# One PSUM pool, tile 0's output projection ahead of tile 1's value sums, one load for the shift and scale weights, and a longer per-tile tail in the last group

## The chip, the cores and the metric

The kernel runs on one core of one Trainium2 chip. The metric is device time in microseconds: the median of three runs of the kernel before is 567.99 us (566.24 to 569.38). Engines are named as in the profile: PE is TensorE (PEld its weight loads), DVE is VectorE, ACT is ScalarE, POOL is GpSimd, SP is SyncE, which here only issues DMAs.

## What is computed

A transformer block with adaptive layernorm on 2048 tokens of width 576, in bf16. From the reference, shortened:

```
mod = silu(c) @ w_mod                      # six rows of 576: sa, ca, ga, sb, cb, gb
h = layernorm(x) * (1 + ca) + sa
x = x + ga * A(h)                          # sliding attention: 32 heads of 18, 8 keys two apart
h = layernorm(x) * (1 + cb) + sb
x = x + gb * ((h @ w_gate) * (h @ w_up)) @ w_down       # 4608 inner columns
```

## The kernel before

Tokens are worked in 16 tiles of 128, two of which make a chunk of 256 for the attention. The feed-forward part runs over five groups of tiles, `GROUPS = [(0, 2), (2, 6), (6, 10), (10, 13), (13, 16)]`; in each, `gate_up` makes the product `hh` of 36 row tiles of the inner width (line L630 for its matmuls), and `down` sums it against `w_down`. The attention of later chunks is cut into pieces and placed between the matmuls of earlier groups. Every engine's order is the order in which the program is written (`manual_schedule`); no planner moves anything. Waits come from the data and from buffers that must be free again.

Three places matter here.

**The start.** `load_wm` loads the weights of one row of `mod` as columns: a 128-partition DMA for four chunks of the width and a 64-partition DMA for the last (L167, L168). It is called twice for `wmA`, for the shift and for the scale of the first layernorm. `mod_columns(wmA, 0)` multiplies them with silu(c) on PE (`pm`, L292: 25 matmuls for the shift, 25 for the scale); between the two stand 16 matmuls on zeros (`run_idle`, L183), whose result nobody reads. The evictions of the first transposes into `hT` need the result (`modc`); the first projections `pq` (L347) read `hT` and the weights `wqk`.

**The hand-over to the first group.** For chunk 0 the weighted values are summed on PE: `av_sum(j, hf)` (L516) sums half of the keys for tile j into three PSUM tiles `po`, and after the second half ACT copies that tile's columns to `oT` (L519 to L521). `b_wj(j)` multiplies them with Wo (`pwj`, L530); its result, called later, lets DVE add the residual and take the statistics of the second layernorm (L536, L537, L240). `rsq2` is that layernorm's Ln and Exp on ACT, `norm2` its normalization on DVE (L250), `transposed(xn2, ...)` its transposes on PE (L277) and their evictions, which split over DVE and ACT and end in `h2T`. Between these stand the projections of chunk 2: `a_q(2, g)` (L347) and `a_v(2, j)` (L373, L375; evicted to `v_sb` by ACT, L377, L378, and stored by POOL). In the kernel before, both tiles' sums stand ahead of Wo of tile 0. The PSUM tiles come from two pools: `pop` with three banks for `po` and the idle matmuls, and a pool of five for all others. Ahead of the first group both are closed and one of eight banks is opened, so that the first `pg` waits until all old banks are released.

**The end.** `down` of the last group has three tiles. For each row tile f of the inner width it runs, for each tile, one matmul of 512 columns into `acc` (two of 256 for the last tile; L697) and one of 64 columns into `accr` (L701). The loop stops at `last`:

```
        last = FT - FB                       # 36 - 4
        for f in range(last):
            for j in range(nj):
                mm_a(f, j)
                mm_r(f, j)
            if f % FB == FB - 1:
                load_wd(gi * NBLK + f // FB + 3)
```

The down weights come in nine blocks of four row tiles (`load_wd`, L164, issued by POOL), through three buffers. Block 8 goes into the buffer of block 5 and is issued after row tile 23. After the loop the remaining row tiles are run by kind: first all `accr` of all tiles, then tile by tile the `acc` (L728), each followed by its multiplication with `gb_bc` on DVE (L729), its addition to the residual (L731; on POOL for the first two tiles, on DVE for the last) and its store (L733).

Of the kernel before, what the change touches and what calls it, by code (L numbers as in the profile page):

```python
# [8 lines left out]
F32 = mybir.dt.float32  # L9
ALU = mybir.AluOpType  # L10
ACTF = mybir.ActivationFunctionType
AX = mybir.AxisListType
PSUM = bass.MemoryType.PSUM
# [5 lines left out]
P = 128  # L19
D = 576  # L20
DP = 640
KT = 5
KF = 4
# [5 lines left out]
FT = FF // P  # L29
# [3 lines left out]
CH = 256  # L33
ST = CH // P
NB = 512
FB = 4
# [7 lines left out]
def kernel(  # L44
# [13 lines left out]
    nc = tc.nc  # L58
# [6 lines left out]
    def pool(name, bufs, **kw):  # L65
        return ctx.enter_context(tc.tile_pool(name=name, bufs=bufs, **kw))
# [18 lines left out]
    wdp = pool("wdp", 3)  # L85
    gup = pool("gup", 3)
    outr = pool("outr", 1)
    guards = [tc.tile_pool(name="pop", bufs=3, space=PSUM), tc.tile_pool(name="psp0", bufs=5, space=PSUM)]
    pop, psp = [g.__enter__() for g in guards]

    def ps(shape, dt, name):
        return psp.tile(shape, dt, name=name, tag="bank")

    def js(j):
        return slice(j * P, (j + 1) * P)
# [70 lines left out]
    def load_k(dst, wsrc, c0, n):  # L166
        r = nc.sync.dma_start(dst(slice(0, P), slice(0, KF)), wsrc[0:KF * P, c0:c0 + n].rearrange("(k p) n -> p k n", p=P))  # L167
        nc.sync.dma_start(dst(slice(0, 64), KF), wsrc[KF * P:D, c0:c0 + n])  # L168
        return r

    def load_wm(wm, bi, blk):
        return load_k(lambda p, k: wm[p, k, bi, :], w_mod, blk * D, D)

    x_in[0] = sp.tile([P, ST, D], BF, name="x_t0")
    for j in range(ST):
        nc.sync.dma_start(x_in[0][:, j, :], x_flat[js(j), :])
    zero = sp.tile([P, P], BF, name="zero")
    nc.vector.memset(zero[:], 0.0)
    idle = pop.tile([P, 2, CH], F32, name="po")

    def run_idle(n):
        for _ in range(n):
            nc.tensor.matmul(idle[:, 0, 0:P], lhsT=zero[:], rhs=zero[:], start=True, stop=True, skip_group_check=True)  # L183

    c_row = sp.tile([KT, P], BF, name="c_row")
    nc.vector.memset(c_row[:], 0.0)
# [11 lines left out]
    wmCr = x1p.tile([P, D], BF, name="x1")  # L198
    nc.gpsimd.memset(wmA[64:, KF, :, :], 0.0)
    nc.gpsimd.memset(wmCr[64:, :], 0.0)  # L200
    load_wm(wmA, 0, 0)
    load_wm(wmA, 1, 1)
    load_k(lambda p, k: wqk[p, k, 0:D], A_wqkv, 0, D)
    load_k(lambda p, k: wqk[p, k, D:DP], A_wqkv, 2 * D - 64, 64)
    load_k(lambda p, k: wqk[p, k, DP:2 * D], A_wqkv, D, D - 64)
# [79 lines left out]
    def mod_columns(wm, pi):  # L285
        pm = ps([P, 2, KT], F32, "pm")
        for bi in range(2):
            if pi == 0 and bi == 1:
                run_idle(16)
            for kt in range(KT):  # L290
                for m in range(KT):
                    nc.tensor.matmul(pm[:, bi, m:m + 1], lhsT=wm[:, kt, bi, col(m)], rhs=sc[:, kt:kt + 1],  # L292
                                     start=(bi == 0 and kt == 0 and m == 0), stop=(kt == KT - 1), skip_group_check=True)
        c01 = slice(2 * pi, 2 * pi + 2)
        nc.vector.tensor_tensor(modc[:, c01, 0:KF], pm[:, :, 0:KF], addc[:, :, 0:KF], ALU.add)
        for r in (slice(0, 64), slice(64, P)):
            nc.vector.tensor_tensor(modc[r, c01, KF:KT], pm[64:P, :, KF:KT], addc[64:P, :, KF:KT], ALU.add)
# [59 lines left out]
    def a_q(i, g):  # L357
        qk_tiles(i, QGRP[g], slice(0, CH), nc.scalar.copy)
        if g == 2:
            a_halo(i)  # L360
# [146 lines left out]

    def av_sum(j, hf):
        if j == 0 and hf == 0:
            pos.extend(pop.tile([P, 2, CH], F32, name="po") for _ in range(3))  # L510
        v = weighted[j][:].rearrange("p w d h -> p w (d h)")
        r = DIL * (W - 1) if j == 0 else 0
        for w in range(4 * hf, 4 * hf + 4):
            sh = DIL * (W - 1 - w)
            for m in range(KT):
                nc.tensor.matmul(pos[m // 2][:, m % 2, j * P:(j + 1) * P + r], lhsT=v[:, w, col(m)], rhs=slide[:, P - sh:2 * P - sh + r],  # L516
                                 start=(j == 0 and w == 0 and m % 2 == 0), stop=(w == W - 1), skip_group_check=True)
        if hf == 1:
            nc.scalar.copy(oT[:, 0:2, js(j)], pos[0][:, :, js(j)])  # L519
            nc.scalar.copy(oT[:, 2:4, js(j)], pos[1][:, :, js(j)])  # L520
            nc.scalar.copy(oT[0:64, KF, js(j)], pos[2][64:P, 0, js(j)])  # L521
# [162 lines left out]
    def down(gi, hh, bg):  # L684
        t0, t1 = GROUPS[gi]
        nj = t1 - t0
        last = FT - FB
        at = spread([(1.0, p) for p in bg], last)
        final = gi == NG - 1
        acc = [ps([P, 512], F32, "acc") for _ in range(nj - final)]  # L690
        halves = [(ps([P, CH], F32, "acc"), slice(CH * h, CH * (h + 1))) for h in range(2)] if final else []
        accr = ps([P, 2 * ST, 64], F32, "accr")

        def mm_a(f, j):
            wb = wd_blk[gi * NBLK + f // FB]
            for a, cs in [(acc[j], slice(0, 512))] if j < len(acc) else halves:
                nc.tensor.matmul(a[:], lhsT=hh[:, f, js(j)], rhs=wb[:, f % FB, cs], start=(f == 0), stop=(f == FT - 1))  # L697

        def mm_r(f, j):
            wb = wd_blk[gi * NBLK + f // FB]  # L700
            nc.tensor.matmul(accr[:, j, :], lhsT=hh[:, f, js(j)], rhs=wb[:, f % FB, 512:D],  # L701
                             start=(f == 0 and j == 0), stop=(f == FT - 1), skip_group_check=True)
# [7 lines that stand above are left out]
            for piece in at[f]:  # L710
                piece()
        xs = [x1[t // ST][t % ST] for t in range(t0, t1)]
        for j in range(nj):
            for f in range(last, FT):
                mm_r(f, j)
        o_ts = [gup.tile([P, 512], BF, name="o_t", tag="g_sb" if j % 2 else "u_sb") for j in range(nj)]
        t_r = outr.tile([P, 2 * ST, 64], BF, name="t_r")
        nc.vector.tensor_tensor(t_r[:, 0:nj, :], accr[:, 0:nj, :],
                                gb_bc[:, None, 512:D].to_broadcast([P, nj, 64]), ALU.mult)
        if final:  # L720
            for j in range(nj):
                nc.vector.tensor_tensor(xs[j][:, 512:D], t_r[:, j, :], xs[j][:, 512:D], ALU.add)
            for j in range(nj):
                r0 = (t0 + j) * P
                for a, cs in [(acc[j], slice(0, 512))] if j < nj - 1 else halves:
                    for f in range(last, FT):
                        wb = wd_blk[gi * NBLK + f // FB]
                        nc.tensor.matmul(a[:], lhsT=hh[:, f, js(j)], rhs=wb[:, f % FB, cs], start=False, stop=(f == FT - 1))  # L728
                    nc.vector.tensor_tensor(o_ts[j][:, cs], a[:], gb_bc[:, cs], ALU.mult)  # L729
                    adder = nc.gpsimd if j < nj - 1 else nc.vector  # L730
                    adder.tensor_tensor(xs[j][:, cs], o_ts[j][:, cs], xs[j][:, cs], ALU.add)  # L731
                    stored = slice(0, CH) if cs.stop == CH else slice(cs.start, D)
                    nc.sync.dma_start(out_flat[r0:r0 + P, stored], xs[j][:, stored])  # L733
            return
        for j in range(nj):
            for f in range(last, FT):
                mm_a(f, j)
            nc.vector.tensor_tensor(o_ts[j][:], acc[j][:], gb_bc[:, 0:512], ALU.mult)
        for j in range(nj):
            r0 = (t0 + j) * P  # L740
            nc.vector.tensor_tensor(xs[j][:, 0:512], o_ts[j][:], xs[j][:, 0:512], ALU.add)
            nc.vector.tensor_tensor(xs[j][:, 512:D], t_r[:, j, :], xs[j][:, 512:D], ALU.add)
            nc.sync.dma_start(out_flat[r0:r0 + P, :], xs[j][:])
        load_wd(gi * NBLK + NBLK + 2)
# [30 lines left out]
    nc.gpsimd.tensor_copy(sc_bc[:], sc[:, :, None].to_broadcast([P, KT, P]))  # L775
    run_idle(24)
    ev = [transposed(xn0, lambda m, j=j: hT0[:, m, js(j)], (j,), 0) for j in range(ST)]
    mod_columns(wmA, 0)
    for e in ev:
        e()  # L780
# [42 lines left out]
    load_x(2)  # L823
    wmB = sp.tile([P, KT, 2, D], BF, name="wmB", tag="wm")
    nc.gpsimd.memset(wmB[64:, KF, :, :], 0.0)
    load_k(lambda p, k: wmB[p, k, :, :].rearrange("p k b n -> p k (b n)") if k != KF else wmB[p, k, :, :].rearrange("p b n -> p (b n)"), w_mod, 3 * D, 2 * D)
    for dd4 in range(4):
        nk = (DH - dd4 + 3) // 4
        wsrc = bass.AP(A_wo.tensor, A_wo.offset + dd4 * D, [[DH * D, H], [4 * D, nk], [1, D]])
# [59 lines left out]
    xn2, stat2, rsq2, norm2 = ln_parts(lambda j: x1[0][j], "b")  # L889
    ht, _ = h2_of(0)  # L890
    a_q(2, 1)
    av_sum(1, 0)
    a_q(2, 2)
    av_sum(1, 1)
    x1_half = b_wj(0)
    x1_half(stat2)
    rsq2(slice(0, 1))
    a_q(2, 3)
    x1_half = b_wj(1)
    norm2(0)  # L900
    x1_half(stat2)
    rsq2(slice(1, 2))
    a_q(2, 4)
    transposed(xn2, lambda m: ht[:, m, js(0)], (0,), 2)()
    norm2(1)
    a_v(2, 0)
    transposed(xn2, lambda m: ht[:, m, js(1)], (1,), 2)()
# [2 lines left out]
    behind(b_ld(1, 1), wgu_in[4])  # L910
    load_res(1)
    load_x(4)
    for guard in [sp_guard] + guards[::-1]:
        guard.__exit__(None, None, None)
    psp = pool("psp", 8, space=PSUM)
    hh0_guard = tc.tile_pool(name="hh0", bufs=1)
    hh0 = hh0_guard.__enter__().tile([P, FT, CH], BF, name="hh")
    sc_bc2 = lnp.tile([P, KT, P], BF, name="ln_xn")
# [68 lines left out]
```

## Time and profile before

| | |
|---|---|
| median of three runs | 567.99 us (566.24 to 569.38) |
| profiled execution | 567.9 us, of which the span is 565.9 us |
| PE busy | 552.2 us (98%) |
| DVE, ACT, POOL busy | 58%, 44%, 12% |
| first `pg` matmul of the first group | 55.54 us |
| first matmul of the per-tile tail (L728) | 557.42 us |
| last DVE addition ends | 562.33 us |

All times inside the execution are counted from the start of the span. A row of a timeline gives start, duration, engine, line, operation, tiles and how many instructions were merged into it, and in brackets how long the engine was idle before it and what ended that.

### The profile page before, as it was taken

Reading aid. Unit: us, or ns where it says so; the run is one execution under the profiler, and the core shown is the slowest. Engines: PE = TensorE matmul, PEld = TensorE weight load, DVE = VectorE, ACT = ScalarE, POOL = GpSimd, SP = SyncE. Lnnn points to the kernel's source line nnn. Section 1 sums busy time; section 2 is a strip of 40 time slices with the busy share of each in tenths; the row PEclk is TensorE's granted clock in tenths of the full one; section 3 lists DMA queues with packets and bytes.
Section 4 is the critical chain, followed back from the end, with each engine's and each line's share of the span. In section 5 each row is a group of like instructions: output and inputs, shape, how many; then the busy total and the mean of one; then the engine's idle time right before and its main releaser. Section 6 shows DMA issues by size and latency. Waiting matters only on the chain.

```text
span 565.9 us, 14371 instructions
## 1 busy us (share of the span) xinstructions
PE 552.2 (98%) x6068; PEld 328.9 (58%) x6068; DVE 327.9 (58%) x788; ACT 250.9 (44%) x576; POOL 70.2 (12%) x105
## 2 busy tenths in 40 slices
PE   7998999999999999999999999999999999999995
PEld 7775887566444445656444445655556555555563
DVE  4976889995767787251867787306736615322203
ACT  3654566254465653333355654230466511555400
POOL 7000401232000001121000100122000022000022
PEclk9998999999999999999999999999999999999999
DMA  9997999849434854382444766347556665565063
GB/s 247 296 290 228 321 288 338 275 135 299 134 115 170 276 172 140 90 278 89 146 136 150 232 201 184 92 135 264 160 179 195 184 194 186 169 209 162 2 176 107
DMA packets 71242, 108.14 MB, mean 191 GB/s; under 512 B 4138, under 2 KB 60538, under 8 KB 71050
## 3 DMA queue, kind: packets, MB, share of 16 engines
q1 hardware_dynamic: 60000, 61.42, 35.6%
q0 software_dynamic: 11168, 45.81, 25.6%
q8 instruction: 47, 0.77, 0.6%
q14 instruction: 17, 0.14, 0.1%
q10 hardware_dynamic: 10, 0.00, 0.0%
HBM read 102.78 MB, written 4.44 MB: 189 GB/s over the span
## 4 chain that ended last, share of the span: by engine, by line
PE 87%; DVE 2%; ACT 1%; issue 0%; ACTq 0%
PE pg L630 27%; PE pu L630 22%; PE acc L697 21%; PE pq L347 4%; PE accr L701 3%; PE pw L547 2%; PE pv L373 2%; PE lg L408 2%; PE tr_pA L277 1%; PE oT_pA L478 0%; PE tr_pB L277 0%; PE pwr L545 0%; PE lt L424 0%; PE acc L728 0%; PE pvr L375 0%
## 5 line engine op out<-in xcount | busy, mean ns | idle before, releaser
L630 PE MATMUL pg<-h2T,wgu 64*128 64x512 bf16 (+2 forms) x1440 | 277.3, 333 | 0.0
L630 PE MATMUL pu<-h2T,wgu 64*128 64x512 bf16 (+2 forms) x1440 | 276.0, 333 | 0.0
L630 PEld LDWEIGHTS <-wgu 64*128 64x128 bf16 x2880 | 141.6, 94 | 106.9 <-issue 0.5
L654 ACT CAST u_sb<-pu 128x512 bf16<-128x512 f32 (+2 forms) x180 | 90.3, 501 | 136.6 <-PE pg L630 133.2
L697 PE MATMUL acc<-wd,hh 128*128 128x512 bf16 (+1 forms) x596 | 146.7, 369 | 0.1
L659 DVE TENSOR_TENSOR hh<-g_sb,u_sb 128x512 bf16<-128x512 bf16 (+2 forms) x180 | 66.8, 373 | 101.5 <-ACT g_sb L655 97.7
L701 PE MATMUL accr<-wd,hh 128*128 128x64 bf16 x576 | 101.1, 193 | 0.0
L655 ACT CAST g_sb<-pg 128x512 bf16<-128x512 f32 (+2 forms) x180 | 91.3, 507 | 0.0
L697 PEld LDWEIGHTS <-hh 128*128 128x128 bf16 x596 | 55.8, 98 | 58.1 <-issue 1.7
L164 POOL DMA_DIRECT2D wd<-in_B_w_down_dram x45 | 33.8, 751 | 279.9 <-PE accr L701 227.2
L630 PE MATMUL pg<-h2T,wgr 64*128 64x512 bf16 (+2 forms) x180 | 60.3, 335 | 0.5 <-ACT v_sb L378 0.5
L630 PE MATMUL pu<-h2T,wgr 64*128 64x512 bf16 (+2 forms) x180 | 60.3, 335 | 0.3 <-ACT u_sb L654 0.3
L701 PEld LDWEIGHTS <-hh 128*128 128x128 bf16 x576 | 52.4, 98 | 2.7 <-issue 0.4
L398 DVE TENSOR_TENSOR prod<-qT,kT 128x1280 bf16<-128x1280 bf16 x56 | 44.8, 819 | 2.5 <-PE lg L408 2.5
L347 PE MATMUL pq<-hT,wqk 128*128 128x256 bf16 (+1 forms) x405 | 45.3, 261 | 0.9 <-ACT hT L268 0.4
L458 DVE TENSOR_TENSOR vsh<-vsh,attn 128x1152 bf16<-128x1152 bf16 x56 | 41.0, 752 | 0.0
L347 PEld LDWEIGHTS <-wqk 128*128 128x128 bf16 x405 | 33.9, 98 | 7.2 <-issue 0.7
L266 DVE TENSOR_SCALAR h2T<-tr_pA,modc 128x256 bf16<-128x256 bf16 (+1 forms) x30 | 9.6, 377 | 36.4 <-PE tr_pA L277 36.4
L392 POOL DMA_DIRECT2D vsh<-vd x14 | 12.7, 905 | 135.8 <-DVE o_sb L469 88.0
L630 PEld LDWEIGHTS <-wgr 64*128 64x128 bf16 x360 | 18.1, 94 | 17.2 <-issue 4.7
L350 ACT CAST qT<-pq 128x512 bf16<-128x512 f32 x16 | 9.3, 583 | 31.2 <-PE pq L347 31.2
L373 PE MATMUL pv<-wv,hT 128*128 128x504 bf16 x80 | 20.7, 391 | 0.1
(160 smaller groups left out, 455.9 us busy)
## 6 DMA issues: line engine op xcount, KB each, us to landing
wd<-in_B_w_down_dram POOLq DMA_DIRECT2D x45, 576.0 KB, 4.6
wgu<-in_B_w_gate_dram SPq DMA_DIRECT2D x45, 512.0 KB, 4.2
wgu<-in_B_w_up_dram SPq DMA_DIRECT2D x45, 512.0 KB, 5.6
vsh<-vd POOLq DMA_DIRECT2D x14, 1152.0 KB, 6.8
x_r<-in_A_x_dram SPq DMA_DIRECT2D x8, 288.0 KB, 7.3
out_dram<-x SPq DMA_DIRECT2D x15, 144.0 KB, 4.4
x_t<-in_A_x_dram SPq DMA_DIRECT2D x7, 288.0 KB, 7.0
vd<-v_sb POOLq DMA_DIRECT2D x14, 144.0 KB, 3.4
```

The lines of the kernel that those rows point to most:

```text
L164: return nc.gpsimd.dma_start(wb[:], B_w_down[r0:r0 + FB * P, :].rearrange("(k p) n -> p k n", p=P))
L347: nc.tensor.matmul(pq[:, gi, :], lhsT=wqk[:, kt, m * P:(m + 1) * P], rhs=hT[:, kt, cols], start=(kt == 0), stop=(kt == KT - 1))
L373: nc.tensor.matmul(pv[:], lhsT=hT[:, kt, js(j)], rhs=wv[:, kt, 0:VA * DH], start=(kt == 0), stop=(kt == KT - 1))
L392: return nc.gpsimd.dma_start(vsh[:].rearrange("p w d h -> p w (d h)"), vsrc)
L398: nc.vector.tensor_tensor(prod[:], aa[i]["qT"][:], aa[i]["kT"][:, :, off:off + CH], ALU.mult)
L458: nc.vector.tensor_tensor(v, v, at, ALU.mult)
L630: return nc.tensor.matmul(bank[:, 0:N], lhsT=lhs, rhs=rhs, start=first, stop=last, skip_group_check=True)
L654: nc.scalar.copy(u[:, 0:N], pu[:, 0:N])
L655: nc.scalar.copy(g[:, 0:N], pg[:, 0:N])
L659: nc.vector.tensor_tensor(hh[:, f, 0:N], gu[0][:, 0:N], gu[1][:, 0:N], ALU.mult)
L697: nc.tensor.matmul(a[:], lhsT=hh[:, f, js(j)], rhs=wb[:, f % FB, cs], start=(f == 0), stop=(f == FT - 1))
L701: nc.tensor.matmul(accr[:, j, :], lhsT=hh[:, f, js(j)], rhs=wb[:, f % FB, 512:D], start=(f == 0 and j == 0), stop=(f == FT - 1), skip_grou ...
```

## The change

Four edits, in one diff:

- All PSUM tiles come from one pool of eight banks in rotation, from the start of the kernel to its end. Idle matmuls and `po` take their banks from it.
- `load_wm2` loads shift and scale weights together: one DMA of 128 partitions with rows of 1152 elements, and one of 64 partitions. The 16 idle matmuls inside `mod_columns` go; 8 stand ahead of it instead.
- Wo of tile 0, its residual, statistics, Ln and Exp stand ahead of tile 1's sums; the projections of chunk 2 are placed anew around them, and the eviction of tile 0's transposes swaps its sides (three on ACT, two on DVE).
- In the last group `last` is `FT - 2 * FB`: eight row tiles per tile are summed after the loop instead of four. All additions there are on DVE.

```
-    guards = [tc.tile_pool(name="pop", bufs=3, space=PSUM), tc.tile_pool(name="psp0", bufs=5, space=PSUM)]
-    pop, psp = [g.__enter__() for g in guards]
+    psp = pool("psp", 8, space=PSUM)
...
+    def load_wm2(wm, blk):
+        for p, k in ((slice(0, P), slice(0, KF)), (slice(0, 64), KF)):
+            dst = wm[p, k, :, :]
+            src = w_mod[0:KF * P, blk * D:(blk + 2) * D].rearrange("(k p) n -> p k n", p=P) if k != KF else w_mod[KF * P:D, blk * D:(blk + 2) * D]
+            nc.sync.dma_start(dst.rearrange("p k b n -> p k (b n)") if k != KF else dst.rearrange("p b n -> p (b n)"), src)
...
-    load_wm(wmA, 0, 0)
-    load_wm(wmA, 1, 1)
+    load_wm2(wmA, 0)
...
         for bi in range(2):
-            if pi == 0 and bi == 1:
-                run_idle(16)
             for kt in range(KT):
...
+    run_idle(8)
     mod_columns(wmA, 0)
...
-        last = FT - FB
+        final = gi == NG - 1
+        last = FT - (2 if final else 1) * FB
...
-                    adder = nc.gpsimd if j < nj - 1 else nc.vector
-                    adder.tensor_tensor(xs[j][:, cs], o_ts[j][:, cs], xs[j][:, cs], ALU.add)
+                    nc.vector.tensor_tensor(xs[j][:, cs], o_ts[j][:, cs], xs[j][:, cs], ALU.add)
...
     a_q(2, 1)
-    av_sum(1, 0)
-    a_q(2, 2)
-    av_sum(1, 1)
     x1_half = b_wj(0)
     x1_half(stat2)
     rsq2(slice(0, 1))
-    a_q(2, 3)
+    av_sum(1, 0)
+    av_sum(1, 1)
+    norm2(0)
+    a_q(2, 2)
     x1_half = b_wj(1)
-    norm2(0)
     x1_half(stat2)
     rsq2(slice(1, 2))
+    a_q(2, 3)
+    transposed(xn2, lambda m: ht[:, m, js(0)], (0,), 2)(False)
     a_q(2, 4)
-    transposed(xn2, lambda m: ht[:, m, js(0)], (0,), 2)()
     norm2(1)
     a_v(2, 0)
     transposed(xn2, lambda m: ht[:, m, js(1)], (1,), 2)()
...
-    for guard in [sp_guard] + guards[::-1]:
-        guard.__exit__(None, None, None)
-    psp = pool("psp", 8, space=PSUM)
+    sp_guard.__exit__(None, None, None)
```

More of the change, by code (lines that the diff above doesn't have):

```diff
@@ L169, in load_k @@
         return r
-    def load_wm(wm, bi, blk):
-        return load_k(lambda p, k: wm[p, k, bi, :], w_mod, blk * D, D)
+    def load_wm2(wm, blk):
[3 more added lines that the diff above has]
+            nc.sync.dma_start(dst.rearrange("p k b n -> p k (b n)") if k != KF else dst.rearrange("p b n -> p (b n)"), src)
     x_in[0] = sp.tile([P, ST, D], BF, name="x_t0")
@@ L178 @@
     nc.vector.memset(zero[:], 0.0)
-    idle = pop.tile([P, 2, CH], F32, name="po")
     def run_idle(n):
+        idle = ps([P, P], F32, "idle")
         for _ in range(n):
-            nc.tensor.matmul(idle[:, 0, 0:P], lhsT=zero[:], rhs=zero[:], start=True, stop=True, skip_group_check=True)
+            nc.tensor.matmul(idle[:], lhsT=zero[:], rhs=zero[:], start=True, stop=True, skip_group_check=True)
     c_row = sp.tile([KT, P], BF, name="c_row")
@@ L509, in av_sum @@
         if j == 0 and hf == 0:
-            pos.extend(pop.tile([P, 2, CH], F32, name="po") for _ in range(3))
+            pos.extend(ps([P, 2, CH], F32, "po") for _ in range(3))
         v = weighted[j][:].rearrange("p w d h -> p w (d h)")
@@ L686, in down @@
         nj = t1 - t0
-        last = FT - FB
+        final = gi == NG - 1
+        last = FT - (2 if final else 1) * FB
         at = spread([(1.0, p) for p in bg], last)
-        final = gi == NG - 1
         acc = [ps([P, 512], F32, "acc") for _ in range(nj - final)]
@@ L825 @@
     nc.gpsimd.memset(wmB[64:, KF, :, :], 0.0)
-    load_k(lambda p, k: wmB[p, k, :, :].rearrange("p k b n -> p k (b n)") if k != KF else wmB[p, k, :, :].rearrange("p b n -> p (b n)"), w_mod, 3 * D, 2 * D)
+    load_wm2(wmB, 3)
     for dd4 in range(4):
```

## Prediction, made before the changed kernel was run

> **What bounds the kernel now.** I read the page first, then the waits of the first 60 us, then the three places that the diff touches (start, hand-over to the first feed-forward group, end), as a timeline and in 1 us windows.
>
> ```profile
> span 565.9 us, 14371 instructions
> PE 552.2 (98%) x6068; PEld 328.9 (58%) x6068; DVE 327.9 (58%) x788; ACT 250.9 (44%) x576; POOL 70.2 (12%) x105
> ```
>
> TensorE (PE) is busy 98% of the span, so the change can gain only where PE idles or runs at a reduced clock. The waits show one large place, tile 1's second layernorm:
>
> ```profile
> PE tr_pA L277 <- DVE ln_xn L250: 2.3, 2, 1.8
> ```
>
> The windows (busy us of PE, PEld, DVE, ACT, POOL; then granted clock, DMA share, GB/s) show what that idle does:
>
> ```profile
> 49.00:50.00 1.00, 0.99 (x9) 0.39 (x6) 0.93 (x4) 0.00 (x0) 0.00 (x0) 1.00 1.11 351
> 50.00:51.00 1.00, 0.00 (x0) 0.00 (x0) 0.96 (x4) 0.27 (x1) 0.00 (x0) 1.00 0.87 283
> 51.00:52.00 1.00, 0.19 (x3) 0.20 (x4) 0.96 (x4) 0.97 (x5) 0.00 (x0) 0.85 0.29 98
> 52.00:53.00 1.00, 1.00 (x7) 0.59 (x6) 0.65 (x3) 1.00 (x5) 0.00 (x0) 0.50 0.12 42
> 53.00:54.00 1.00, 1.00 (x4) 0.31 (x3) 1.00 (x3) 0.74 (x3) 0.54 (x1) 0.50 0.05 18
> 54.00:55.00 1.00, 1.00 (x7) 0.49 (x6) 0.66 (x1) 0.21 (x1) 0.00 (x0) 0.50 0.38 148
> 55.00:56.00 1.00, 0.51 (x11) 0.54 (x12) 0.00 (x0) 0.49 (x2) 0.21 (x1) 0.95 0.00 0
> ```
>
> After 1.8 us of idle the clock is 0.50 for about 3.4 us; (0.15 + 3 x 0.50 + 0.05) = 1.7 us of full-speed time is the price of one such drop. The timeline shows it in the same five matmuls, and what starts the first group:
>
> ```profile
> 48.47 1.22 PE L373 MATMUL pv<-wv,hT 128*128 128x504 bf16 x5
> 51.81 0.50 PE L277 MATMUL tr_pA<-ident,ln_xn 128*128 128x128 bf16 x3 [1.82 <-DVE ln_xn L250]
> 52.49 2.26 PE L373 MATMUL pv<-wv,hT 128*128 128x504 bf16 x5
> 55.54 0.27 PE L630 MATMUL pg<-h2T,wgr 64*128 64x256 bf16 x1 [0.49 <-ACT v_sb L378]
> ```
>
> At the end VectorE (DVE) runs late, with GpSimd (POOL) adding beside it:
>
> ```profile
> 551.64 0.75 POOL L164 DMA_DIRECT2D wd<-in_B_w_down_dram  x1 [1.62 <-PE accr L701]
> 557.04 0.54 PE L701 MATMUL accr<-wd,hh 128*128 128x64 bf16 x13
> 557.42 2.76 PE L728 MATMUL acc<-wd,hh 128*128 128x512 bf16 x16
> 560.40 1.27 DVE L731 TENSOR_TENSOR x<-o_t,x 128x256 bf16<-128x256 bf16 x1
> 562.04 0.29 DVE L731 TENSOR_TENSOR x<-o_t,x 128x256 bf16<-128x256 bf16 x1
> ```
>
> The first line issues the last block of down weights (block 8, row tiles 32 to 35). Its own landing answer:
>
> ```profile
> DMA to landing us min/median/max: 5.4/5.4/5.4
> ```
>
> So it lands at 551.64 + 5.4 = 557.0, when PE first wants it (557.07, the second of the 13): slack nil.
>
> **The sum is made against the profiled execution: 567.9 us, 2.0 outside its span of 565.9.** The median of the three runs shown is 567.99, the same within 0.1.
>
> **Middle: tile 0's Wo ahead of tile 1's sums.** No PE work is added; the same matmuls stand in another order. Both versions agree until PE leaves a_q(2,1) at 40.42. From there, with starts taken from the rows of before: Wo of tile 0 takes 1.22 (43.20 to 44.42), to 41.64; tile 1's two half sums 1.12 each (40.42 to 41.53), to 43.88; a_q(2,2) 0.55, to 44.43. DVE begins tile 0's residual and statistics 0.88 after Wo starts, at 41.30, and needs 2.74 (44.08 to 46.82), to 44.04. On ScalarE (ACT) the Ln and Exp of that tile now stand ahead of tile 1's three oT copies, which PE's second Wo waits for, with a_q(2,3) and all later PE work behind it: the copies start at 44.5 and end at 44.9, 45.2 and 45.4. PE waits 0.5, and Wo of tile 1 ends at 46.2. Then a_q(2,3) 1.1, transposes 0.3, a_q(2,4) 1.1, a_v(2,0) 1.5: 50.2. DVE meanwhile starts tile 1's half at 45.9, ends at 48.6, and after Ln and Exp norm2(1) is done at 49.85, ahead of PE: the 1.82 idle is gone and with it the clock drop. Transposes 0.3 and a_v(2,1) 1.5 bring PE to 52.1. What is late next is ACT: from Exp (49.1) it has two kT copies (0.46 each), three tr_pA evictions (0.35 each; one more than the two it had, since the eviction sides are swapped), v_sb (0.57) and two tr_pB evictions (0.35 each): h2T's last chunk, which the first gate matmul reads, is there at 52.4. With one PSUM pool the first group no longer waits for every bank to be released (the 0.49 on v_sb). It starts at 52.5 in place of 55.54: **-3.0**. In parts: idle 1.8, clock 1.4 (3.25 us from 51.81 to 55.05 against 1.85), pool hand-over and small gaps 0.7, less new waits of 0.9. From here every group is PE-bound, so the gain stays; the value loads on POOL behind v_sb come earlier too. Bounds: -1.5, if ACT's order costs as much again, to -3.4, if its new waits vanish.
>
> **End: eight row tiles per tile, additions on DVE.** PE work is the same: four row tiles more (28 to 31) move out of the loop. Without a new wait: DVE needs 0.69 (L729) and, for a 128x512 bf16 add, 0.37 (the hh product's row) per tile, 1.06 under 8 x 0.216 = 1.73 of PE, so DVE keeps up; the two POOL adds (1.15 each, nothing else queued there) and the 1.27 add that ran beside them (0.29 alone) go. PE's last matmul ends at 560.18 as before; 0.04, then 0.41 and 0.29 of DVE with 0.03 between: 560.97 in place of 562.33, -1.36. The four stores follow their adds on SP at least 0.7 apart, and one issue takes 0.36: no queue.
>
> But the load of block 8 stays where it was (after row tile 23, when block 5's buffer is free), while its first reader moves ahead by four row tiles: the loop leaves at 557.07 - 4 x 0.742 = 554.10, four accr matmuls (0.029 each) run, and the fifth, row tile 32 of tile 0, needs block 8 at 554.2. Everything left on PE stands behind it: 20 accr, 16 of 0.216, 16 of 0.109 = 5.8 us. The wait is 557.0 - 554.2 = 2.8 with this trace's landing, 1.8 with the 4.4 that is usual for this load. I take the middle, **+2.3**. It idles PE longer than the 1.82 that dropped the clock at 50, and 5.8 us of work follow, room for the whole drop: up to 1.7, less what of it falls into the wait; I take **+1.4** (0 to 1.7). Together -1.36 + 2.3 + 1.4 = **+2.3** (bounds +0.4 to +3.1).
>
> [...]
>
> **Start: shift and scale weights in one load.** In place of two pairs of DMAs there is one pair; SP issues two fewer (0.58 and 0.52) and all behind them (wqk, wv, x) can be issued 1.1 earlier. The rows:
>
> ```profile
> 9.37 0.69 PEld L292 LDWEIGHTS <-wmA 128*128 128x128 bf16 x25 [0.42 <-DMA wmA<-in_w_mod_dram]
> 11.64 0.23 PEld L347 LDWEIGHTS <-wqk 128*128 128x128 bf16 x4 [0.53 <-DMA wqk<-in_A_wqkv_dram]
> ```
>
> Before, 25 of the pm matmuls were done while the second half was on its way; now all 50 wait, 25 more x 0.03 = +0.7 if the last byte comes when it came. Against it: the DMA engines are at 0.9 or more from 2 us on, so bytes set the time, and one pair has no issue gaps; and L347 waits for wqk anyway, which no pm delay under 0.5 moves. I take **0** (-0.5, the wqk wait, to +0.7). The idle matmuls moved ahead of pm cost nothing while PE would wait there; their 8 in place of 16 leave PE idle up to 1 us.
>
> **One PSUM pool elsewhere.** No PE wait of the first 36 us is for a bank; **0** (-0.2 to +0.5, the longest PE wait for an eviction elsewhere, pwr on oT).
>
> **Sum:** 567.9 - 3.0 + 2.3 + 0 = **567.2**.
>
> **Rivals.**
> 1. The clock holds through the wait at the end, so that only -1.36 + 2.3 = +0.9 is left there: -3.0 + 0.9, 565.8. It decides whether a wait of this length is enough for a drop. For: waits of 0.5 did not drop it. Against: 1.8 did. Chance 0.17. [...]
> 2. Block 8 lands in time: -3.0 - 1.4 = 563.5. It would have to land 2.5 us after issue; none of 45 loads took less than 4.3. Chance 0.06.
> 3. Slower: the clock stays at 0.50 for a second 3.4 us, because the stretch in which PE resumes begins with idle. Place: the 5.8 us after block 8's landing; price 1.7 more, with the late landing: -3.0 - 1.36 + 2.8 + 3.4 = +1.8, 569.7 (572.1 if all 5.8 us run at half). [...] Against: at 55 one such stretch sufficed. Chance 0.10.
> 4. ACT's order eats half of the middle gain: -1.5 + 2.3, 568.7. Chance 0.10.
> 5. PE's idle before pm drops the clock for the first projections: +1.7, 568.9. Chance 0.07.
>
> **How the numbers follow.** The forecast has 0.50. Half a percent is 2.8 us, about what a measurement of this kernel tells from no change. Faster than 565.1: rival 2, nearly half of rival 1 at its bounds, and a little of the forecast: 0.20. Slower than 570.7: most of rival 3, and tails of 4 and 5 with a full drop: 0.15. Same: 0.65. The range runs from rival 1 with the short wait and the middle at its best (564.6) to rival 3 (569.8).
>
> **What would show it.** After: no PE wait for ln_xn over 0.6 near 50; clock 1.00 from 49 to 56; first L629 matmul at 52.5. PE idle of 1.8 to 2.8 about 551 (span times less 3.0), ended by wd's landing, clock 0.50 behind it; no POOL add; the last DVE add 0.5 us behind the last matmul. Wrong: no wait for wd there, or the first gate matmul at 54 or later.

## The result, and the profile after

The changed kernel's median is 566.46 us over 13 runs (564.67 to 568.1), against 567.99 for the kernel before in the same session. The ratio is 0.9962, with a 95% interval of 0.9944 to 0.9980: 0.38% faster, or 2.2 us (1.1 to 3.2). That is within the half percent that the prediction called the same; its forecast, 567.2, is 0.7 too high. As a gain it forecast 0.7 (567.9 to 567.2), and 2.2 were measured. The profiled execution took 566.68 us, with a span of 564.8. The engines' part of the page:

```profile
span 564.8 us, 14311 instructions
PE 548.9 (97%) x6023; PEld 327.6 (58%) x6060; DVE 327.9 (58%) x789; ACT 250.9 (44%) x577; POOL 67.1 (12%) x103
```

PE shows 3.3 us less work than before in a span only 1.1 shorter, so 2.2 us more of the span are without a row of PE. Not all of that is idle time: PE has 37 matmul rows fewer than weight loads, so some records are missing, and its gaps of up to 0.25 us add up to 3.0 here and to 1.3 before.

**The middle.** The stretch that stood at clock 0.50 before, in the same windows as those of before (busy us of PE, PEld, DVE, ACT, POOL, then granted clock, DMA share, GB/s):

```profile
49.00:50.00 1.00, 1.00 (x7) 0.49 (x6) 0.86 (x4) 0.97 (x4) 0.00 (x0) 1.00 1.11 350
50.00:51.00 1.00, 1.00 (x15) 0.69 (x13) 0.51 (x3) 1.00 (x4) 0.00 (x0) 1.00 1.10 351
51.00:52.00 1.00, 0.91 (x9) 0.53 (x8) 1.00 (x3) 1.00 (x4) 0.00 (x0) 1.00 0.66 217
52.00:53.00 1.00, 0.19 (x4) 0.19 (x5) 0.92 (x2) 1.00 (x4) 0.54 (x1) 1.00 0.30 103
53.00:54.00 1.00, 1.00 (x22) 1.00 (x20) 0.00 (x0) 0.35 (x2) 0.36 (x1) 1.00 0.49 183
```

The clock is 1.00 throughout, ACT is busy the whole of 50 to 53, and PE's idle has moved to 52, where it is half as long. The waits of the first 60 us name what is late now:

```profile
PE pg L629 <- ACT h2T L269: 0.9, 1, 0.9
PE tr_pA L278 <- DVE ln_xn L251: 0.5, 1, 0.5
```

The wait of 1.8 for the second layernorm is gone from its place (the 0.5 left is at 33, ahead of an earlier tile's transposes), and the first group waits for ACT's last eviction into `h2T`. The timeline has the new start of that group, and the wait ahead of the second Wo:

```profile
45.24 1.47 PE L529 MATMUL pwj<-wo,oT 128*128 128x288 bf16 x10 [0.33 <-ACT oT L518]
52.81 0.27 PE L629 MATMUL pg<-h2T,wgr 64*128 64x256 bf16 x1 [0.91 <-ACT h2T L269]
```

The first gate matmul starts at 52.81, against 55.54 before and 52.5 predicted.

**The end.** The timeline from block 8's load on:

```profile
550.40 0.75 POOL L163 DMA_DIRECT2D wd<-in_B_w_down_dram  x1 [1.62 <-PE accr L700]
554.80 0.74 PE L700 MATMUL accr<-wd,hh 128*128 128x64 bf16 x20 [1.65 <-DMA wd<-in_B_w_down_dram]
555.60 5.15 PE L727 MATMUL acc<-wd,hh 128*128 128x512 bf16 x31
561.24 0.29 DVE L729 TENSOR_TENSOR x<-o_t,x 128x256 bf16<-128x256 bf16 x1
```

PE now waits 1.65 for the block, which landed 4.4 after its issue (5.4 before). POOL's additions are gone. The last one of DVE ends at 561.54, 0.8 behind PE's last matmul (560.75); before it was 2.15 behind. In the windows of the wait the clock does not move:

```profile
553.00:554.00 1.00, 0.16 (x6) 0.06 (x3) 0.00 (x0) 0.00 (x0) 0.00 (x0) 1.00 0.89 359
554.00:555.00 1.00, 0.20 (x7) 0.19 (x7) 0.00 (x0) 0.00 (x0) 0.00 (x0) 1.00 0.05 18
555.00:556.00 1.00, 0.95 (x21) 0.68 (x19) 0.38 (x2) 0.00 (x0) 0.00 (x0) 1.00 0.00 0
```

**Between.** One more wait is in this trace, in the third group:

```profile
390.31 0.63 PE L700 MATMUL accr<-wd,hh 128*128 128x64 bf16 x16 [1.39 <-DMA wd<-in_B_w_down_dram]
```

That block took 9.2 from issue (381.10) to landing, with value loads moving beside it. No other trace of this study has this wait, that of e8 below, which is the changed kernel again, included, so I count it as an accident of this execution and not as part of the change.

All traces can be cut in the same way: the start, up to the first `po` matmul; the middle, from there to the first `pg`; the groups, up to the last `accr` of row tile 27 in the last group; and the end, from there to the last DVE addition. In us:

| kernel | start | middle | groups | end | span |
|---|---|---|---|---|---|
| before | 36.81 | 18.73 | 498.55 | 8.24 | 565.9 |
| after | 37.14 | 15.67 | 500.04 | 8.69 | 564.8 |
| difference | +0.33 | -3.06 | +1.49 | +0.45 | -1.1 |

The middle gives what was forecast. It is paid back in three places, one of which is the accident. The 0.33 of the start comes from the value weights `wv`: the projections `pq` start 0.59 earlier than before, but behind them PE waits 0.81 for `wv`. The row of before, then two of after:

```profile
11.65 5.51 PE L347 MATMUL pq<-hT,wqk 128*128 128x128 bf16 x90 [0.35 <-DVE hT L266]
11.06 5.48 PE L346 MATMUL pq<-hT,wqk 128*128 128x128 bf16 x90
17.35 1.22 PE L372 MATMUL pv<-wv,hT 128*128 128x504 bf16 x5 [0.81 <-DMA wv<-in_A_wqkv_dram]
```

The experiments separate the parts and ask how often the clock drops.

### The profile page after: what moved, and what is told of

Its sections match the earlier page's. It is cut to its first block, busy times and chain, and to the rows that moved or that the text cites. A ratio compares the mean times of both kernels' runs of the same rounds, so it can differ in the third digit from the quotient of the medians.

```text
span 564.8 us, 14311 instructions
## 1 busy us (share of the span) xinstructions
PE 548.9 (97%) x6023; PEld 327.6 (58%) x6060; DVE 327.9 (58%) x789; ACT 250.9 (44%) x577; POOL 67.1 (12%) x103
## 4 chain that ended last, share of the span: by engine, by line
PE 56%; issue 28%; DMA 6%; DVE 4%; POOL 2%; ACT 2%; SPq 0%; POOLq 0%; ACTq 0%; DVEq 0%
PE pg L629 17%; PE pu L629 14%; PE acc L696 10%; PE pq L346 5%; DMA wd<-in_B_w_down_dram 2%; POOL wd L163 2%; PE accr L700 2%; PE pv L372 2%; PE pw L546 2%; DMA wv<-in_A_wqkv_dram 1%; PE lg L407 1%; DMA vd<-v_sb 1%; DMA wmA<-in_w_mod_dram 1%; PE tr_pA L278 1%; PE acc L727 1%
## 5 line engine op out<-in xcount | busy, mean ns | idle before, releaser
L696 PE MATMUL acc<-wd,hh 128*128 128x512 bf16 (+1 forms) x550 | 138.9, 369 | 0.2
L700 PE MATMUL accr<-wd,hh 128*128 128x64 bf16 x576 | 99.2, 193 | 4.5 <-DMA wd<-in_B_w_down_dram 3.0
L696 PEld LDWEIGHTS <-hh 128*128 128x128 bf16 x580 | 54.5, 98 | 57.1 <-issue 1.7
L700 PEld LDWEIGHTS <-hh 128*128 128x128 bf16 x576 | 51.7, 98 | 5.8 <-issue 3.6
L464 DVE TENSOR_TENSOR vsh<-vsh 128x1152 bf16<-128x1152 bf16 x28 | 20.5, 751 | 0.0
```

What stands on the lines that cost most here:

```text
L464: nc.vector.tensor_tensor(vsh[:, d], vsh[:, d], vsh[:, 4 + 2 * s:6 + 2 * s], ALU.add)
```

## The experiments

The theory: the middle is worth -3, the wait for block 8 takes the end's gain back and a clock drop behind it may add to that, and the start costs something, against the forecast of nothing. The rivals: the middle's gain is only the clock drop (then the order would bring nothing where the clock holds), or the start is free, and the pay-back is all at the end.

**The middle alone, the end alone, the start alone.** Each is the kernel before with one part of the diff.

```
e1: the PSUM pool and the order of the hand-over, as in the diff
e2: -        last = FT - FB
    +        last = FT - (2 if final else 1) * FB
    -                    adder = nc.gpsimd if j < nj - 1 else nc.vector
    -                    adder.tensor_tensor(...)
    +                    nc.vector.tensor_tensor(...)
e3: -    load_wm(wmA, 0, 0)
    -    load_wm(wmA, 1, 1)
    +    load_wm2(wmA, 0)
    -            if pi == 0 and bi == 1:
    -                run_idle(16)
    +    run_idle(8)
         mod_columns(wmA, 0)
```

> The kernel before with the one PSUM pool and the new order around tile 0's Wo; start and end are those of before. Theory (the middle carries the gain, by its idle and the clock drop behind it): first gate matmul near 52.5 us, PE wait for ln_xn near 50 under 0.6, clock 1.00 throughout; time 3.0 less than before, 565.0. Rival (the single load at the start carries it): the time stays within 1 us of before.

> The kernel before with eight row tiles per tile summed at the end and DVE additions; start and middle are those of before. Theory (PE waits for block 8): a PE wait of 1.6 to 2.8 us ended by wd's landing, last DVE addition 0.4 to 1.4 later than without the edit when the clock holds (568.4 to 569.4), up to 1.7 more when it drops. Rival (the edit is a gain that other things in the changed kernel hide): no wait, 1.4 less, 566.6.

> The kernel before with shift and scale weights in one load and 8 idle matmuls ahead of them. Theory (DMA engines are the limit there, so what comes earlier for the first projections is given back at the value weights): first projection 0.6 earlier, wait for wv 0.5 to 0.9 longer, a_q(2,0) within 0.4 of before; time within 0.5 of before, 567.5 to 568.5. Rival (the start carries the gain): a_q(2,0) a microsecond or more earlier, 566.5.

| kernel | median us | ratio to before (95%) | start | middle | groups | end |
|---|---|---|---|---|---|---|
| e1, middle | 565.1 | 0.9941 (0.9923 to 0.9960) | 37.77 | 15.67 | 498.65 | 8.25 |
| e2, end | 569.38 | 1.0026 (1.0006 to 1.0047) | 37.35 | 17.69 | 498.57 | 11.31 |
| e3, start | 569.0 | 1.0023 (1.0006 to 1.0040) | 38.51 | 17.69 | 498.50 | 8.25 |

The middle brings its whole 3 us, alone: 0.59% is 3.35 us (2.3 to 4.4). The other two parts each make the kernel slower. Two of the middle stages here, 17.69, belong to the order of before: in e2 and e3 the same PE idle of 1.8 stands ahead of tile 1's transposes, and no drop follows. 18.73 - 17.69 = 1.04 is therefore what the drop cost in the trace of before, where I had put 1.4. The order's own gain is there without it.

In e2's trace the drop comes at the end instead, behind a wait of 2.6. Its timeline and windows:

```profile
556.53 1.01 PE L701 MATMUL accr<-wd,hh 128*128 128x64 bf16 x20 [2.61 <-DMA wd<-in_B_w_down_dram]
```

```profile
556.00:557.00 1.00, 0.47 (x14) 0.46 (x14) 0.00 (x0) 0.00 (x0) 0.00 (x0) 0.91 0.00 0
557.00:558.00 1.00, 0.78 (x12) 0.63 (x11) 0.39 (x2) 0.00 (x0) 0.00 (x0) 0.50 0.00 0
558.00:559.00 1.00, 1.00 (x3) 0.29 (x2) 0.37 (x3) 0.00 (x0) 0.00 (x0) 0.50 0.00 0
559.00:560.00 1.00, 1.00 (x4) 0.39 (x3) 0.00 (x0) 0.00 (x0) 0.00 (x0) 0.50 0.00 0
560.00:561.00 1.00, 1.00 (x6) 0.41 (x5) 0.30 (x1) 0.00 (x0) 0.00 (x0) 0.88 0.00 0
```

This is the end as the forecast drew it: block 8 lands 5.3 after issue, PE waits, and the matmuls behind it run at 0.50 for 3.4 us. It costs 11.31 - 8.24 = +3.1, the upper bound of that step. The timed runs show that it is not always so. A stretch of 3.4 us at 0.50 takes 0.003 off a run's mean granted clock, by an estimate from this trace (half of 3.4 over a span of 567.7). e2's twelve runs fall apart by that mean: four at 0.999 or 1.000 took 566.7 to 568.3, four at 0.996 took 568.7 to 569.9, four at 0.993 or 0.994 took 570.8 to 571.1. Steps of 1.5 to 1.7 between the groups' medians, as whole drops would make them (half of 3.4 is 1.7). The mean alone does not say at which place a run had them, and a stretch begun at the kernel's end takes a little off it too: in the trace of before the clock is 0.50 from 563.70 to the span's end at 565.9, 0.002 by the same estimate.

In e3 the projections were expected 0.6 earlier and the time within 0.5 of before; neither came. The start has a wait that was not there before, and then what rival 5 described:

```profile
9.42 1.67 PE L292 MATMUL pm<-sc,wmA 128*128 128x1 bf16 x50 [1.06 <-DMA wmA<-in_w_mod_dram]
```

```profile
12.00:13.00 1.00, 1.00 (x13) 1.00 (x11) 1.00 (x6) 0.86 (x3) 0.25 (x1) 0.50 1.10 267
13.00:14.00 1.00, 1.00 (x12) 1.00 (x11) 0.30 (x2) 0.00 (x0) 0.00 (x0) 0.50 1.08 350
14.00:15.00 1.00, 1.00 (x12) 1.00 (x11) 0.00 (x0) 0.27 (x1) 0.00 (x0) 0.50 1.10 357
```

All 50 `pm` matmuls stand behind one pair of DMAs, which landed at 9.37 and 10.06 here; before, half of them ran on a pair that lands at 6 to 7.5, and only the second half waited, for a pair landing at 9.33 and 9.70. The merged load comes no earlier than the second of the two that it replaces. PE idles 1.06, and the first projections start 0.71 later than before (12.36 against 11.65) and run at half clock.

**More idle matmuls at the start.** If the start's cost is the clock drop, keeping PE fed through the wait should remove it.

```
e5, on e3:  -    run_idle(8)
            +    run_idle(24)
```

> The single load at the start as in the start-only kernel, but 24 idle matmuls ahead of the pm matmuls in place of 8, so that TensorE is busy 1.0 us longer while the load is on its way. Theory A (the edit's cost is the clock drop that TensorE's idle brings at the first projections): no clock of 0.50 between 8 and 16 us, po starts 0.5 to 1 earlier than in the start-only kernel's trace (38.5), time within 0.5 of before. Theory B (the cost is the later landing of the one load): cost stays, 569.

The drop went, and the start of the trace with it: 36.72, as before's 36.81. The first window of the projections has 18 matmuls where e3 has 13:

```profile
12.00:13.00 1.00, 0.97 (x18) 0.97 (x18) 0.73 (x3) 0.28 (x1) 0.00 (x0) 1.00 1.15 293
```

Its load also landed earlier than e3's, at 9.05 and 9.49. But in e10 (below), where it landed at 9.06 and 9.48 behind 8 idle matmuls, the projections ran at half the rate, so the 24 matmuls are the likelier reason. Over twelve runs the kernel still is at 568.86, ratio 1.0015 (1.0004 to 1.0027), not within 0.5 us of before as expected. So a cost of the start remains on average that this trace does not show. I take the start as +0.1% to +0.4% with its 8 matmuls, and leave open how much of it is the clock.

**The middle's two halves.** One run each.

> The kernel before with one PSUM pool and nothing else. From the first po matmul to the first gate matmul before took 18.73 with a clock drop and 17.69 without. Theory (the pool only spares the hand-over wait for all banks): 0.3 to 0.5 less than the one of these that its clock matches. Rival (the order alone does all): the same as before.

> The kernel before with the new order around tile 0's Wo, but its two PSUM pools and their closing. Theory (order gives the idle, pool the hand-over): from first po to first gate matmul 15.67 plus 0.3 to 0.9, since the first gate matmul waits for tile 1's v_sb; no TensorE wait for ln_xn over 0.6. Rival (five banks are too few for the new order): new TensorE waits on evictions, 17 or more.

| kernel | us | middle |
|---|---|---|
| before, with the drop | 567.99 | 18.73 |
| e6, pool alone, with the drop | 567.49 | 18.04 |
| e7, order alone | 565.15 | 16.36 |
| e1, both | 565.1 | 15.67 |

The two add up: the pool is worth 0.69 (18.73 - 18.04, and again 16.36 - 15.67), the order 1.33 without a drop (17.69 - 16.36) and the drop 1.04 where it comes. e7's waits still have the one that the second pool causes:

```profile
PE pg L630 <- ACT v_sb L378: 0.6, 1, 0.6
```

**Block 8 read later.** To take away what makes PE wait at the end, without moving the load: rows 28 to 31 of the first two tiles, and all tiles' `accr` of these rows, run ahead of anything that reads block 8.

```
e4, on after:
+        if final:
+            for j in range(nj - 1):
+                for f in range(last, FT - FB):
+                    mm_a(f, j)
+            for j in range(nj):
+                for f in range(last, FT - FB):
+                    mm_r(f, j)
         for j in range(nj):
-            for f in range(last, FT):
+            for f in range(FT - FB, FT):
                 mm_r(f, j)
...
-                    for f in range(last, FT):
+                    for f in range(FT - FB if j < nj - 1 else last, FT):
```

> The changed kernel, with row tiles 28 to 31 of tiles 0 and 1 and of all the 64-column parts run ahead of the first reader of block 8 (2.1 us of PE work). Theory (the wait for block 8 is what the end lost): no PE wait at the end, last addition 1.5 earlier than in the changed kernel, 565.0. Rival (DVE is the limit at the end): the wait goes but DVE ends the kernel where it did, 566.5.

In the trace the wait for block 8 is gone and the end takes 7.97, although PE now waits 0.66 for block 7, which landed 5.62 after its issue (4.70 before). That wait also hides one for block 8, which landed at 556.46, just when PE came to it:

```profile
PE acc L696 <- DMA wd<-in_B_w_down_dram: 0.7, 1, 0.7
```

Over twelve runs it is 566.7, ratio 0.9968 (0.9948 to 0.9987): no better than the change itself. Its trace says where the end's gain went in that execution: the start idles 1.53 for `wmA`, which landed at 9.84 and 10.51, the clock falls at 11.51, and the first `po` stands at 39.04 in place of 37.14. So a combination with the start of before was worth a kernel (e9, below).

**A longer wait.** The load of block 8 four row tiles later in the program, to see whether a longer idle drops the clock.

```
e8, on after:
-            if f % FB == FB - 1:
+            if f % FB == FB - 1 and not (final and f == 5 * FB + 3):
                 load_wd(gi * NBLK + f // FB + 3)
+            if final and f == 6 * FB + 3:
+                load_wd(gi * NBLK + NBLK - 1)
```

> The changed kernel with the load of block 8 issued after row tile 27 in place of 23, three microseconds later. Theory (the wait is the landing of this load, and the clock drops when it is long enough): the wait at the end grows from 1.65 by 2.97 to 4.3 to 5.6, the clock falls to 0.50 for at least 3.4 us after it, last DVE addition 4.0 to 5.0 later than in the changed kernel's trace, counted from the end of row tile 27. Rival (the clock is not ruled by idle here): 3.0 later, clock 1.00.

The edit did not move the load. POOL reaches it early and waits only for the buffer, so the issue still came 2.45 ahead of the end of row tile 27, and the kernel is the changed one again. It serves as a second trace of that one: block 8 took 5.2 to land, the wait was 2.4, and the clock stayed at 1.00.

```profile
554.00:555.00 1.00, 0.00 (x0) 0.00 (x0) 0.00 (x0) 0.00 (x0) 0.00 (x0) 1.00 0.68 277
555.00:556.00 1.00, 0.00 (x0) 0.00 (x0) 0.00 (x0) 0.00 (x0) 0.00 (x0) 1.00 0.10 41
556.00:557.00 1.00, 0.74 (x21) 0.68 (x21) 0.02 (x1) 0.00 (x0) 0.00 (x0) 1.00 0.00 0
```

e2's wait was 2.6 and its clock fell. The end took 9.52, +1.28 against before; with -1.36 for DVE and the wait of 2.4 the prediction's sum gives +1.04. Its time, 568.09, has another part in the start, where the first `po` is at 39.26. The rows of `pq` there, with the wait for `wmA` in front:

```profile
9.23 1.73 PE L291 MATMUL pm<-sc,wmA 128*128 128x1 bf16 x50 [0.85 <-DMA wmA<-in_w_mod_dram]
12.91 6.73 PE L346 MATMUL pq<-hT,wqk 128*128 128x128 bf16 x90
```

The 90 matmuls take 5.48 in the trace of after. Here they run 12 to a microsecond up to 16.1, the rate of e3 at clock 0.50, although the clock column says 1.00: this trace has no record of the clock before 16.13, and without one the column reads 1.00.

**Four row tiles, additions on DVE.** Whether eight are needed once POOL no longer adds.

```
e10, on after:  -        last = FT - (2 if final else 1) * FB
                +        last = FT - FB
```

> The changed kernel with four row tiles at the end instead of eight, additions still all on DVE. Theory (at four row tiles DVE needs 1.12 per tile against 0.86 of PE, so DVE is late, but no wait for block 8 arises): no TensorE wait for wd, from the end of row tile 27 to the last DVE addition 8.0 to 8.3, last matmul 1.5 or more before the last addition. Rival (the DVE additions alone shorten the end): 7.5 or less.

One run: 567.38, with the first `po` at 39.12, as late as in e8, and an end of 8.74. Of it 0.7 is a wait for block 7, which was not expected: that block landed 5.62 after its issue, as in e4. Without the wait 8.1 would be left, against 8.24 before. DVE is late: the last matmul ends at 560.23, and the last rows of DVE are

```profile
559.60 0.68 DVE L728 TENSOR_TENSOR o_t<-acc,gb_bc 128x512 bf16<-128x512 f32 x1
561.77 0.29 DVE L729 TENSOR_TENSOR x<-o_t,x 128x256 bf16<-128x256 bf16 x1
```

so its end lies 1.83 behind PE, where eight row tiles make it 0.8. Four tiles give DVE 0.87 of PE work for each 1.06 of its own; the eight are what lets it follow.

**The middle and the end that reads late, with the start of before.**

```
e9: e1's pool and order, e2's end, e4's late reads, the start of the kernel before
e11: e1 again, beside it on the same chip
```

> The start of before, the middle of the changed kernel (one pool, new order), and at the end eight row tiles with block 8 read late as in the late-read kernel. Theory (each stage's cost adds up and the end is free of waits when block 7 and 8 land in 4.4): from the end of row tile 27 to the last DVE addition 6.9 to 8.0 against 8.25, first gate matmul as in the middle-only kernel; time 0.3 to 1.3 under the middle-only kernel's 565.1, so 563.8 to 564.8, the fastest so far. Rival (the loads' landing varies as much as the new tail needs): 8.0 or more at the end, time as middle-only.

> The middle-only kernel again, beside the kernel with the middle and the late-read end. Theory: 565.1 again (564 to 566), first gate matmul 15.67 after the first po matmul, end stage 8.25. Rival (its first result was a lucky chip): within 1 us of before.

e9 is the fastest: 564.06 over six runs (562.88 to 564.58), ratio 0.9928 (0.9913 to 0.9944), and it beats both kernels. e11 is at 565.13, ratio 0.9949 (0.9936 to 0.9963). The stages of e9's trace are 37.01, 15.66, 498.48 and 7.78; the only wait left at the end is one for block 8, which landed 5.25 after its issue:

```profile
PE accr L700 <- DMA wd<-in_B_w_down_dram: 0.6, 1, 0.6
```

The late reads are worth 0.2% on top of the middle by these ratios (8.25 - 7.78 = 0.47 us in the traces; the intervals overlap). By their code e9 and e4 differ in the start alone, up to the load of `wmB`, which is the same two DMAs in both: 0.9928 against 0.9968, each to the kernel before beside it, 0.4% or 2.3 us, with an interval of about 1.5 either way (the half widths 0.0016 and 0.0020 put together as independent).

## Why the prediction came out as it did

**The middle, -3.0, was right, and its steps with it.** Measured: -3.06 in the traces of after and of e1. Tile 1's layernorm is no longer waited for; ACT is next, with 0.33 at the second Wo (0.5 forecast) and 0.91 at `h2T` (0.4 forecast, from 52.1 to 52.5); the hand-over of the pools gives 0.69 (0.7 forecast for it and small gaps). Two sizes were off in ways that cancelled: the drop is 1.04 and not 1.4, and the reordering brings 1.33 after its new waits, a little more than the 1.8 - 0.9 of the sum. Rival 4 (ACT's order eats half of it) is out: the middle is 15.66 or 15.67 in after, e1, e4, e8, e9 and e11. What I did not see is that before itself does not have the drop in every execution: the same idle of 1.8 dropped the clock in the traces of before and e6 (2.22 there), and not in e2, e3 and e5. The gain of the middle is thus 2.0 or 3.1 in one execution.

**The end had the right mechanism and a term of the sum mis-sized.** DVE keeps up, POOL's additions are gone, and PE waits for block 8. The wait was taken from the middle of 1.8 and 2.8 as 2.3; it was 1.65, 2.4 and 2.6 in three traces, because the landing took 4.4, 5.2 and 5.3. The clock drop, +1.4 in the forecast, came in e2's trace and not in those of after and e8; rival 1 (the clock holds, +0.9 left) is what after's profile shows, with +0.45. Of the 13 runs of after, six had a mean clock of 0.998 or 0.999 and took 565.4 in the median, five had 0.996 or 0.997 and took 566.5; two at 1.000 took 567.9 and 568.1, like e8 with its late clock at the start. So in some executions a drop may well be there. The step of the prediction, which took any wait over 1.8 as enough for a drop, does not hold: e2's clock dropped after 2.6 of idle, and e8's did not after 2.4. Rival 3 (a second stretch at 0.50) and rival 2 (block 8 lands in time) were in no trace; the shortest landing of that block was 4.4, in after. Of the signs that the prediction named, the distance of DVE's last addition from PE's last matmul, 0.5, disagrees with its own terms, which give 0.79 (560.97 - 560.18); 0.8 was measured.

**The start was the step that failed.** I took 0, between -0.5 and +0.7, on two arguments: bytes set the landing, and L347 waits for `wqk` anyway. The first is not what decides: the whole load lands where the second half landed, within 8.2 to 10.5 from trace to trace, so nothing of `pm` can run early and its 50 matmuls and the eviction behind them are late together. The second holds only for a delay under 0.5, as the step itself said: the first `pq` stood at 11.65 before and at 12.36 in e3. How much that costs is a matter of the clock. In the seven traces with the start of before the first `po` stands at 36.77 to 37.77, 37.2 in the mean. In the five with the one load and 8 idle matmuls it stands at 37.14 (after), 38.51 (e3), 39.04 (e4), 39.12 (e10) and 39.26 (e8), 38.6 in the mean. In the last four PE idles 0.67 to 1.53 for `wmA`, and the first projections run at 12 to 13 matmuls to a microsecond, the rate at clock 0.50, where after has 22. That is rival 5, which had 0.07 of the chance; e3's runs put its average at 0.23% (0.06 to 0.40), some 1.3 us. The trace of after does not show it: there the load landed earlier than in any of the four, at 8.16 and 8.93, PE idled 0.26 and 0.20, and the +0.33 is the wait for `wv`. So after's own profile hides the cost that the four others with its start show; what makes the landing differ stays open.

**The sum.** Terms from the traces of after: +0.33 - 3.06 + 0.45, and 1.39 of the 1.49 for the late block in the third group, make -0.9; 0.1 more in the groups and -0.3 behind the last DVE addition make the span's -1.1. By the timed parts it is -3.3 (middle) + 1.5 (end) + 1.3 (start) = -0.5, against -2.2 (-3.2 to -1.1) measured for the whole; each part's interval is about 1 us either way, that of the sum about 1.8, so that sum and whole are not shown to differ. How the drops are shared out among the three places from one execution to the next isn't settled. By luck the forecast of 567.2 stood near the result: a drop at the end that was counted in full and came only at times (+1.4) and a start that was counted at nothing (+1.3) are about the same size. The low end of the range, 564.6, is not the sum of the terms named for it either: 567.9 - 3.4 - 1.36 + 1.8 is 564.9.

## What to carry to other kernels

When a reader is moved ahead of a load, set its new time against the time from issue to landing of that load, and move only the part of the work that does not need it: the late reads kept the longer tail's benefit and shortened its wait to 0.6. Two loads whose first half fed work early were not improved here by one load that landed with the second. An idle of 1.8 in the middle was followed by 3.4 us at clock 0.50 in the trace of before and by none in those of e2, e3 and e5, so a single profile showed one of two outcomes; price such a drop as a chance, and read the mean clock of the timed runs to see how often it came.

## What the runs showed of the hardware that was not expected

**In before and after the granted clock changed at multiples of 3.413 us, and an idle of one length was not followed by a drop in every trace.** The clock records of before begin at 7.32 and change at 51.70, 55.11 and 563.70. The steps are 44.37, 3.41 and 508.59, which is 13, 1 and 149 times 3.413 (508.59 / 149). Those of after begin at 7.36 and change once, 556.37 later, 163 times it. By the 1 us windows the stretch at 0.50 lasts 3.4 in e1 (from 29.80), e2 (556.82), e3 (11.72), e4 (11.52) and e6 (52.18) as well. Laid on in steps of 3.413 from the changes in the same trace (in e8 from 16.13, where its records begin), the stretches around the long idles were busy by these shares:

| kernel | idle of PE | stretch (or the two that share it) | PE busy | clock after it |
|---|---|---|---|---|
| before | 49.99 to 51.81 | 48.28 to 51.70 | 0.47 | 0.50 |
| e6 | 50.09 to 52.31 | 48.77 to 52.18 | 0.39 | 0.50 |
| e2, end | 553.92 to 556.53 | 553.41 to 556.83 | 0.24 | 0.50 |
| e2, middle | 50.53 to 52.34 | cut at 51.65 | 0.64, 0.55 | 1.00 |
| e3, middle | 51.69 to 53.50 | cut at 52.69 | 0.67, 0.54 | 1.00 |
| e5, middle | 49.90 to 51.71 | not placed: clock 1.00 throughout 0 to 58 | | 1.00 |
| after, end | 553.16 to 554.81 | cut at 553.49 | 0.89, 0.60 | 1.00 |
| e8, end | 553.80 to 556.20 | cut at 555.44 | 0.52, 0.76 | 1.00 |

In these rows the stretches busy 0.47 or less were followed by 0.50, and those busy 0.52 or more were not. After an idle of 1.8 in the middle the clock was 0.50 in the trace of before and 1.00 in those of e2, e3 and e5; the idle of 2.6 at the end of e2, which fell whole into one stretch, was followed by 0.50, and that of 2.4 in e8, in two stretches, was not. That it is the place of the idle in these steps which made the difference is my reading of the rows; no run varied the place alone.

**Three stretches that were busier were followed by a drop too.** e1's from 26.38 to 29.80 had PE busy 0.83 of the time:

```profile
29.00:30.00 1.00, 1.00 (x41) 0.97 (x39) 0.92 (x3) 0.50 (x3) 0.00 (x0) 0.90 0.99 211
30.00:31.00 1.00, 1.00 (x4) 0.30 (x2) 0.90 (x5) 0.89 (x2) 0.00 (x0) 0.50 1.06 243
```

In it stand 48 of the 50 `pm` matmuls of one column (1.20 us of PE by their rows) and others of 32 columns. The stretches ahead of the drops at the start, busy 0.65 in e3 and 0.52 in e4, also hold the 50 of one column. Whether the number of columns has to do with these drops is not shown: no run varied it alone. So the busy share by itself does not tell when the clock falls.

**One load's landing time differed by 0.8 with nearly the same program around it:** block 8's 576 KB took 4.4 and 5.2 in after and e8, which have practically the same order of work, 5.4 in before, 5.3 in e2 and 5.25 in e9.
